# A two-layer transformer block: 64-row tile pairs in the first MLP matmul and the q/k/v projections, and a planner that charges tiling changes

## The chip, the cores and the metric

The kernel runs on one core of one Trainium2 chip. The metric is the device time of one execution in microseconds (us), from the first instruction to the last. The engines are called PE (matrix multiply; PEld is its weight loading), DVE (vector), ACT (activation functions), POOL (general) and SP (here: DMA queues only). PE multiplies a stationary operand of up to 128 rows by 128 columns with a moving operand that streams through it column by column; a matmul can also use a tile of the array: 64 of the 128 rows (64x128), 32 rows (32x128), or 32 of the columns (128x32).

## The reference

All tensors are bfloat16; `x` is 2048 rows of 576. Two layers of attention and MLP, each with the same weights:

```python
def _A_ref(x, wqkv, wo):            # 32 heads of 18, window of 256
    qkv = (x @ wqkv).reshape(B, S, 3, H, Dh).transpose(2, 0, 3, 1, 4)
    q, k, v = qkv[0], qkv[1], qkv[2]
    scores = einsum("bhqd,bhkd->bhqk", q, k) * (Dh ** -0.5)
    mask = (idx[:, None] - idx[None, :] >= 0) & (idx[:, None] - idx[None, :] < W)
    p = softmax(where(mask, scores, -1e9))
    o = einsum("bhqk,bhkd->bhqd", p, v)
    return o.transpose(0, 2, 1, 3).reshape(B, S, D) @ wo

def _B_ref(x, w1, b1, w2, b2):      # 576 -> 4608 -> 576
    h = gelu(einsum("bsd,df->bsf", layernorm(x), w1) + b1)
    return einsum("bsf,fd->bsd", h, w2) + b2

x = x + _A_ref(layernorm(x), wqkv, wo);  x = x + _B_ref(layernorm(x), w1, b1, w2, b2)
x = x + _A_ref(layernorm(x), wqkv, wo);  x = x + _B_ref(layernorm(x), w1, b1, w2, b2)
```

The contraction of the projections and of the first MLP matmul is 576 = 4 x 128 + 64, so it is four whole row blocks of the array and a half one.

## The kernel before

**Tiling.** The 2048 rows are 16 row tiles of 128, four row tiles make a chunk, and two layers make 16 / 4 x 2 = 8 chunks (`CH`, `k` = 0 to 7). Per chunk the stages are: layer norm and a transposing DMA into `xnTa` (`ln1`, `ln_norm_T`); q, k and v for each row tile (`qkv`); attention for eight groups of four heads (`E`, with `scores` and `pv`); the output projection, residual and second layer norm (`tail`, into `xnTm`); the first MLP matmul with gelu (`G_part`); the second MLP matmul (`mm2`). The MLP's 36 blocks of 128 features are done in three parts of twelve (`NPT`, `NFH`), so there are 24 calls of `G_part` and 24 of `mm2`. `hT` holds the twelve blocks of one part and is not doubled: the first MLP matmul of a part writes it through gelu, the second reads it.

**q/k/v and output projection.** `two_out` makes one row tile's 576 output columns as two halves of 288 (`HB`), each in a PSUM bank of its own, with five matmuls of 128 rows: the fifth row block has 64 rows of data and 64 rows of zeros (`wqkv[64:128, 4, :]` is zeroed at the start, and `xn` beyond column 576 too).

**First MLP matmul.** Per six feature blocks `G_part` first issues a task called `rest` (line 919): six matmuls of 64 rows each, the half row block of features 0, 3, 1, 4, 2, 5, where 0, 1, 2 lie in rows 0 to 63 of the array and 3, 4, 5 in rows 64 to 127. It opens six PSUM banks. Then each feature block gets its four whole row blocks (line 931) in its bank, and ACT applies gelu to it (line 934). To have the last 64 rows of `xnTm` in both row halves, `ln_norm_T` with `dup=True` writes them twice (line 648). After each sixth feature block a load of the next six blocks of `w1` is queued on SP (`w1_load`: one large DMA and two small; three buffers).

**Order.** Nothing is ordered by hand. `Plan.add` collects tasks with an engine, a cost, resources and a priority; `Plan.schedule` then plays them through in a model and puts each engine's instructions in the order of their planned starts. At each step it takes the task with the smallest key (start, priority, index). PE's tasks have a mode: "f" full tiles (`two_out`, `mm2`, the four whole row blocks, transposes), "h" the 64-row `rest`, "r" the 32-row scores, "c" the 32-column p·v. A task whose mode differs from the one before costs `SWITCH` = 0.095 more in the model, but the key doesn't see this. `rest` tasks may be drawn ahead by up to `HOLD` = 0.3 us. Scores and first MLP matmuls follow one fixed order ("pa"), and so do their activations on ACT ("act"); all else goes by priority. `PL.nudge` adds a number to the priority of each stage ("ea3" is the first part of attention of chunk 3, "q3.1" is q/k/v of its row tile 1, "gb2" the second MLP part of chunk 2, "+" their loads).

`Sched.add` turns resources into semaphore waits. Where a PE task writes what an earlier PE task wrote, no wait is made, since PE keeps the order of its own matmuls:

```python
lw = self.last_write.get(w)
if lw is not None and not (eng == "pe" and lw[2] == "pe"):
    want(lw)
```

PSUM has eight banks. Scores take pairs (0,1), (2,3), (4,5); q/k/v, output projection, `mm2` and p·v take one of 4 to 7 (q/k/v of chunk 1: bank 6); the first MLP matmul may take any.

Of the kernel before, what the change touches and what calls it, by code (L numbers as in the profile page):

```python
# [40 lines left out]
class Sched:  # L41
# [23 lines left out]
    def add(self, eng, fn, reads=(), writes=(), dma=None, ring=4):  # L65
# [11 lines left out]
        for w in writes:  # L77
            for rd in self.readers.get(w, ()):
                if rd[2] != eng or rd[3]:
                    want(rd[:3])  # L80
            lw = self.last_write.get(w)
            if lw is not None and not (eng == "pe" and lw[2] == "pe"):
                want(lw)
# [19 lines left out]
        own = None if dma is not None else eng  # L103
        ev = (c, c.val, own)
# [4 lines left out]
        for r in reads:  # L109
            self.readers.setdefault(r, []).append((c, c.val, own, dma is not None))  # L110
# [49 lines left out]
class Task:  # L160
    __slots__ = ("idx", "eng", "fn", "reads", "writes", "cost", "lat", "prio", "dma", "ring", "handles", "alloc", "move", "desc",
                 "npred", "succ", "ready", "end", "plain", "fifo", "hold", "stage", "mode")
# [24 lines left out]
class Plan:  # L187


    def __init__(self, S, nbanks):  # L190
        self.S = S
        self.tasks = []
        self.lw = {}
        self.rd = {}
        self.nbanks = nbanks
        self.warm_fn = None
        self.warm_from = 0.0
        self.warm_until = 0.0
        self.feed_until = 0.0
        self.hold = 0.0  # L200
        self.ring = RING
        self.stage = ""
        self.nudge = {}
        self.fifo_last = {}

    def add(self, eng, fn, reads=(), writes=(), dma=None, ring=4, cost=0.1, lat=0.1, prio=0.0, alloc=(), fifo=None, plain=False, after=(), move=0.0, desc=0, hold=False, mode="f"):
        stage = self.stage + ("+" if dma in ("w1", "w2", "xr") else "")
# [3 lines left out]
                 plain=plain, move=move, desc=desc, fifo=fifo, hold=hold, stage=stage, mode=mode)  # L211
# [31 lines left out]
    def keep_warm(self, a, b, bank_free, extra):  # L243
# [5 lines left out]
        if n < 1 or not banks:  # L249
            return  # L250
        h = Bank(())
        h.no = banks[0]
        t = Task(idx=-1, eng="pe", fn=lambda e: self.warm_fn(e, h.no, n), reads=("warm",), writes=(h,), cost=n * 0.115, lat=0.1, prio=0.0,
                 dma=None, ring=4, alloc=(), handles=(), plain=False, move=0.0, desc=0, fifo=None, hold=False, stage="", mode="f")
        extra.append((a, t))

    def schedule(self):
# [56 lines left out]
        while len(order) < n:  # L314
            best = None
            cands = []
            for e in ENGS:
                for t in released[e]:
# [7 lines left out]
                    key = (round(st, 3), t.prio, t.idx)  # L326
                    if e == "pe" and (st < self.feed_until or t.mode != "f"):
                        cands.append((key, t, st, got))
# [9 lines left out]
            if t.eng == "pe" and t.fifo is None:  # L338
                for c in cands:
                    if c[1].hold and c[2] <= st + self.hold:  # L340
                        _, t, st, got = c
            if t.eng == "pe" and mode != "f" and t.mode == "f":
                near = [c for c in cands if c[1].mode in "rc" and c[2] <= st + GLUE]
                if near:
                    _, t, st, got = min(near, key=lambda c: c[0])
# [49 lines left out]
            for s, data in t.succ:  # L395
                same = s.eng == t.eng == "pe"
# [7 lines left out]
        for st, t in order:  # L404
            names = lambda rs: [n for r in rs for n in ([f"pb{b}" for b in r.banks()] if isinstance(r, Bank) else [r])]
            if t.plain:
                self.S.plain(t.eng, t.fn)
            else:
                self.S.add(t.eng, t.fn, names(t.reads), names(t.writes), dma=t.dma, ring=t.ring)
# [6 lines left out]
GLUE = -1  # L416
WARM_UNTIL = 140.0
FEED_UNTIL = 40.0
HOLD = 0.3


def build_kernel(nc, A_x, A_wqkv, A_wo, B_x, B_w1, B_b1, B_w2, B_b2, out):
# [25 lines left out]
    PAT = (6, 6)  # L448
# [3 lines left out]
    TOPF = D - 512  # L452

# [9 lines left out]
    PL.nudge = {"b": 29.4, "ea0": -2.66, "ld0": 0.01, "ld0+": -29.79, "eb0": 0.53, "ec0": 3.31, "le0+": 114.63, "q1.0": -118.82, "q1.1":  # L463
                -98.11, "q1.2": -0.91, "q1.3": -7.44, "t0": -5.22, "ea1": -89.48, "ga0": -171.5, "ga0+": 5.04, "eb1": -15.16, "ma0": 12.04,
                "ma0+": -17.91, "gb0": -145.98, "ec1": -2.99, "le1+": 16.44, "le1": -20.83, "mb0": -3.03, "q2.1": 45.54, "q2.2": 88.61,
                "q2.3": 55.86, "t1": -120.53, "gc0": -19.84, "gc0+": -25.1, "ln3": 57.08, "mc0": 4.28, "mc0+": 148.11, "ga1": -4.06, "ga1+":
                -6.33, "eb2": -3.01, "ma1": 5.64, "ma1+": 13.09, "gb1": -0.44, "ec2": 3.21, "mb1": 7.94, "mb1+": -24.34, "q3.0": 14.13,
                "q3.1": 131.09, "q3.2": 4.89, "q3.3": 1.84, "t2": -15.58, "gc1": 7.36, "gc1+": -31.57, "mc1": 17.31, "mc1+": -1.81, "ga2":
                -27.48, "ga2+": 158.23, "eb3": 36.01, "ma2": 50.85, "ma2+": 24.11, "gb2": 23.88, "gb2+": 71.77, "ec3": -0.31, "mb2": 60.21,
                "mb2+": -145.98, "q4.0": 0.58, "q4.1": 63.81, "q4.2": 55.53, "t3": 61.03, "gc2": 154.1, "gc2+": 8.93, "ln5": 14.44, "ea4":  # L470
                19.04, "mc2": 63.19, "ga3": 18.64, "ga3+": 0.44, "eb4": 14.59, "ma3": 30.2, "ma3+": 0.16, "gb3": -9.23, "gb3+": -6.16,
                "mb3": 45.14, "q5.0": 113.74, "q5.1": 29.89, "q5.2": -8.93, "q5.3": 76.56, "t4": -2.66, "gc3": 88.61, "gc3+": -48.97, "ln6":
                -15.57, "ea5": -72.82, "mc3": -2.47, "mc3+": 76.5, "ga4+": -33.16, "eb5": 2.91, "ma4": 29, "ma4+": 17.98, "gb4": -4.52,
                "gb4+": -7.43, "mb4": 59.81, "mb4+": -8.12, "q6.0": 1.38, "q6.1": 19.98, "q6.2": -18.44, "q6.3": 63.81, "gc4": 92.87,
                "gc4+": 84.52, "ln7": 31.11, "ea6": -2.66, "mc4": 24.73, "mc4+": 0.51, "ga5": 11.4, "ga5+": 1.49, "eb6": -0.34, "ma5":
                52.45, "ma5+": -6.49, "gb5": -32.33, "gb5+": 51.26, "ec6": -3.2, "mb5": 0.24, "mb5+": -3.62, "q7.0": 24.18, "q7.2": 137.8,
                "q7.3": 1.6, "t6": -24.34, "gc5": 5.59, "gc5+": -171.5, "ea7": 41.87, "mc5": 136.49, "mc5+": -1.6, "ga6": -32.64, "eb7":
                31.31, "ma6": 44.85, "ma6+": -1.66, "gb6": 0.02, "gb6+": -4.59, "ec7": -0.12, "mb6": 104.87, "mb6+": 63.38, "t7": -16.91,
                "gc6+": -0.75, "mc6": -119.39, "mc6+": -8.02, "ga7": -61.44, "ga7+": -11.43, "ma7": -14.13, "ma7+": 9.77, "gb7": 1, "mb7":
                3.96, "mb7+": -8.3, "gc7": 53.28, "mc7": 65.68, "": 0.88}  # L480
# [92 lines left out]
    def w_load(n, reads=()):  # L573
# [3 lines left out]
        dma("act", wqkv[0:64, 4, n * D:(n + 1) * D], A_wqkv[512:576, n * D:(n + 1) * D], reads=reads, writes=[f"w{w}B"], cost=0.6, prio=-10,  # L577
            fifo="act")
# [13 lines left out]
    add("pool", lambda e: e.memset(xn[:, :, D:KD * 128], 0.0), writes=[f"xn{i}" for i in range(NXN)], cost=0.4, prio=-10)  # L592
# [4 lines left out]
    add("dve", lambda e: e.memset(wqkv[64:128, 4, :], 0.0), writes=["wqC", "wkC", "wvC"], cost=1.0, prio=-8)  # L597
# [15 lines left out]
    PL.hold = HOLD  # L613
# [104 lines left out]
    def qkv(k, i, prio0):  # L718
        l, t0, nt = CH[k]
        A = l * NT + t0 + i  # L720
        for n, w in enumerate("qkv"):
            prio = prio0 + (0.8 if k == 1 and w == "v" else 0.0) if k else QK0.get((w, i), -0.55 + 0.01 * i)
            dest = [f"v{A % VS}h{o}" for o in range(2)] if w == "v" else [f"qn{qn_ctr[0] % NQN}h{o}" for o in range(2)]
            bs = two_out(lambda c: xnTa[:, c, i * 128:(i + 1) * 128], lambda c, s, n=n: wqkv[:, c, n * D + s:n * D + s + HB],
                         [f"w{w}A", f"w{w}B", f"w{w}C", f"xa{i}"], prio + 0.01 * n, after=dest, fill=(6,) if k == 1 else FILL)
# [98 lines left out]
    def pv(k, g, units, bo, first, last, prio):  # L824

        l, t0, nt = CH[k]
        T0 = l * NT + t0

# [29 lines left out]
    def E(k, gs, prio):  # L858
# [3 lines left out]
        for g in gs:  # L862
            units = []
            bo = Bank(OUT)
            for n, parts in enumerate(us):
                units.append((parts, scores(k, g, parts, prio)))
# [6 lines left out]
        for p in pend:  # L873
            pv(k, *p[1:], prio - 0.1)

# [10 lines left out]
    def tail(k, prio):  # L886
        l, t0, nt = CH[k]
        for i in range(nt):
            t = t0 + i
            bs = two_out(lambda c, i=i: attT[:, c, i * 128:(i + 1) * 128], lambda c, s: wo_sb[:, c, s:s + HB],  # L890
# [5 lines left out]
            ln_norm_T(t, i, xnTm[:, k % 2], f"xm{k % 2}_", prio, dup=True)  # L896


    def G_part(k, hf, prio):
# [5 lines left out]
        for n4 in PAT:  # L905
            fs = range(f, f + n4)
            f += n4
            sls = [(k * NGR + ff // GS) % NB1 for ff in fs]
            bks = [Bank(MM1) for _ in fs]
            rd = [[f"w1a{sl}", f"w1b{sl}_0", f"w1b{sl}_1"] for sl in sls]  # L910

            def rest(e, sls=sls, bks=bks):

                ins = None
                for i in (0, 3, 1, 4, 2, 5):
                    sl, bk = sls[i], bks[i]
                    b = i // 3
                    col = 4 * GW + i % 3 * 128
                    ins = e.matmul(bank(bk)[:, 0:n], w1_sb[64 * b:64 * b + 64, sl, col:col + 128], xnTm[64 * b:64 * b + 64, k % 2, 4, 0:n],  # L919
                                   start=True, stop=False, tile_position=(64 * b, 0))  # L920
                return ins
            add("pe", rest, reads=list(dict.fromkeys(sum(rd, []))) + TXm, writes=bks, cost=mm_cost(n) * (n4 // 2) + 0.02, hold=True, mode="h", prio=prio,
                alloc=bks, fifo="pa", after=[f"h{ff - hf * NFH}" for ff in fs])
            for ff, sl, bk, r in zip(fs, sls, bks, rd):
                fl = ff - hf * NFH

                def fn(e, ff=ff, sl=sl, bk=bk):
                    ins = None
                    for c in range(4):
# [216 lines left out]
```

## Time and profile before

| what | value |
|---|---|
| time, three runs | 895.59, 895.8, 897.97 us; median 895.8 |
| span of the profiled execution | 895.5 us |
| granted PE clock, mean | 0.998 |
| ACT busy: exp (L798) / gelu (L934) | 345.8 / 197.8 us |
| ACT table loads | 25 and 24, 1.28 us each |
| second MLP matmul (L960), steps | 2304 of 288 columns, 309.5 us busy |
| output projection (L699, `wo_sb`) | 320 matmuls, 42.8 us busy |
| DMA | 122.25 MB, mean 137 GB/s |

"Busy" counts the time in which an engine has at least one instruction running. On PE that is little help by itself: matmuls overlap, the recorded length of one (287 ns for 288 columns) is longer than the step from its start to the next one's, and a busy engine may be between two tilings. The rows of a group name its source line; a line such as L699 is that of a helper which several stages use, so the operands (`wqkv` or `wo_sb`) tell them apart. A few matmul records are missing from the trace (1100 of 1152 on L931).

### The profile page before, as it was taken

What the parts mean: (1) busy time and instruction counts of PE and PEld (TensorE: products, weight loads), DVE (VectorE), ACT (ScalarE), POOL (GpSimd) and SP (SyncE); (2) the same over time, 40 slices, a digit from 0 to 9 for tenths busy, and PEclk for the clock granted to TensorE, in tenths of its full rate; (3) what the DMA queues carried; (4) which work ended last, traced back from release to release, by engine and by line L of the source; (5) the groups of instructions that cost most, each with busy time, mean ns of one, the idle gap of its engine ahead of it and who ended that gap; (6) DMA issues with size and microseconds to landing.
All of it is one profiled execution on the core that took longest, in us unless ns stands there. A gap on an engine that the chain in (4) does not pass through costs nothing.

```text
span 895.5 us, 19577 instructions
## 1 busy us (share of the span) xinstructions
PE 864.4 (97%) x7849; PEld 506.5 (57%) x7901; DVE 410.1 (46%) x969; ACT 615.8 (69%) x737; POOL 366.2 (41%) x504
## 2 busy tenths in 40 slices
PE   5898999999999999999999999999999999999998
PEld 4555455656566565665655655556556545556665
DVE  6789223863357351763427633375134523161111
ACT  3976888577767788366773868747777689844443
POOL 3677544274244662224431544416444266231100
PEclk9999999999999999999999999999999999999999
DMA  6788537742477333853457342682537632446431
GB/s 177 139 172 173 179 119 182 178 109 81 149 166 158 120 120 98 183 124 121 130 119 181 71 158 86 143 198 67 165 119 147 184 125 71 144 126 176 153 96 50
DMA packets 182649, 122.25 MB, mean 137 GB/s; under 512 B 107424, under 2 KB 181024, under 8 KB 182560
## 3 DMA queue, kind: packets, MB, share of 16 engines
q1 hardware_dynamic: 179152, 115.47, 49.5%
q0 software_dynamic: 1584, 3.54, 1.5%
q10 hardware_dynamic: 1824, 1.99, 0.7%
q8 instruction: 63, 1.03, 0.5%
q14 instruction: 26, 0.21, 0.1%
HBM read 91.28 MB, written 2.36 MB: 105 GB/s over the span
## 4 chain that ended last, share of the span: by engine, by line
PE 54%; DVE 1%; issue 1%; DMA 1%; ACT 1%; POOL 0%
PE ps L960 21%; PE ps L931 18%; PE ps L699 6%; PE ps L789 3%; PE ps L919 3%; PE ps L834 3%; ACT pT L798 1%; DVE x_res L880 0%; DMA xnTa<-xn 0%; DVE st_all L620 0%; DMA xnTm<-xn 0%; DVE xn L643 0%; DVE xn L648 0%; POOL rstd L633 0%; DVE xn L883 0%
## 5 line engine op out<-in xcount | busy, mean ns | idle before, releaser
L819 POOL TENSOR_SCALAR_AFFINE_SELECT pT<-pT 128x512 bf16<-128x512 bf16 (+1 forms) x368 | 283.5, 794 | 266.6 <-ACT pT L798 262.0
L798 ACT ACTIVATE pT<-ps 128x1024 bf16<-128x1024 f32 (+2 forms) x384 | 345.8, 972 | 58.3 <-PE ps L789 57.8
L934 ACT ACTIVATE hT<-ps,b1col 128x512 bf16<-128x512 f32 x288 | 197.8, 687 | 192.8 <-PE ps L931 188.3
L960 PE MATMUL ps<-w_sb,hT 128*128 128x288 bf16 x2304 | 309.5, 287 | 0.2
L960 PEld LDWEIGHTS ps<-w_sb,hT 128*128 128x128 bf16 x2304 | 213.9, 98 | 81.9 <-issue 24.9
L931 PE MATMUL ps<-xnTm,w_sb 128*128 128x512 bf16 x1100 | 255.0, 380 | 4.9 <-issue 3.2
L931 PEld LDWEIGHTS ps<-xnTm,w_sb 128*128 128x128 bf16 x1152 | 109.6, 98 | 137.0 <-issue 19.1
L880 DVE TENSOR_TENSOR x_res<-ps,x_res 128x288 f32<-128x288 f32 x216 | 95.9, 448 | 169.0 <-PE ps L960 158.4
L699 PE MATMUL ps<-wqkv,xnTa 128*128 128x288 bf16 x960 | 136.0, 289 | 3.5 <-DVE qn L742 1.9
L845 DVE STREAM_TRANSPOSE oq<-ps 128x512 f32<-128x512 f32 x64 | 45.8, 715 | 179.0 <-PE ps L834 178.8
L699 PEld LDWEIGHTS ps<-wqkv,xnTa 128*128 128x128 bf16 x960 | 88.4, 98 | 41.4 <-issue 7.8
L742 DVE CAST qn<-ps 128x288 bf16<-128x288 f32 x120 | 53.2, 449 | 35.1 <-PE ps L699 33.0
L942 POOL TENSOR_TENSOR x_res<-x_res,b2bc 128x576 f32<-128x576 f32 x32 | 40.8, 1274 | 69.2 <-ACT hT L934 69.2
L789 PE MATMUL ps<-qT,kT 32*128 32x384 bf16 (+2 forms) x1216 | 64.1, 276 | 2.2 <-ACT pT L798 2.0
L631 POOL TENSOR_SCALAR vtmp<-mv_all 128x1 f32<-128x1 f32 (+1 forms) x43 | 8.5, 197 | 121.4 <-DVE mv_all L622 120.6
L834 PE MATMUL ps<-pT,vA 128*20 128x384 bf16 (+2 forms) x1408 | 50.7, 276 | 2.0 <-ACT pT L798 0.9
L620 DVE BATCH_NORM_STATS2 st_all<-x_res 128x6 f32<-128x288 f32 x104 | 44.8, 448 | 1.2
L919 PE MATMUL ps<-xnTm,w_sb 64*128 64x512 bf16 x288 | 39.7, 381 | 5.5 <-ACT pT L798 3.3
L789 PEld LDWEIGHTS ps<-qT,kT 32*128 32x128 bf16 x1216 | 19.5, 92 | 44.1 <-issue 25.1
L699 PE MATMUL ps<-wo_sb,attT 128*128 128x288 bf16 x320 | 42.8, 286 | 0.1
L834 PEld LDWEIGHTS ps<-pT,vA 128*20 128x20 bf16 x1408 | 25.7, 90 | 26.8 <-issue 13.4
L729 DVE CAST vA<-ps 128x288 bf16<-128x288 f32 x64 | 28.8, 454 | 23.7 <-PE ps L699 23.4
(47 smaller groups left out, 347.6 us busy)
## 6 DMA issues: line engine op xcount, KB each, us to landing
w_sb<-in_B_w_dram SPq DMA_DIRECT2D x48, 864.0 KB, 5.4
w_sb<-in_B_w_dram SPq DMA_DIRECT2D x48, 768.0 KB, 4.7
w_sb<-in_B_w_dram SPq DMA_DIRECT2D x96, 48.0 KB, 4.4
x_res<-in_A_x_dram POOLq DMA_DIRECT2D x3, 1152.0 KB, 7.0
out_dram<-xn SPq DMA_DIRECT2D x16, 144.0 KB, 1.8
wqkv<-in_A_wqkv_dram ACTq DMA_DIRECT2D x3, 576.0 KB, 6.9
w_sb<-in_A_x_dram SPq DMA_DIRECT2D x2, 576.0 KB, 4.2
wo_sb<-in_A_wo_dram SPq DMA_DIRECT2D x4, 144.0 KB, 2.6
```

The lines of the kernel that those rows point to most:

```text
L699: ins = e.matmul(bank(bs[o])[:, 0:HB], lhs(c), rhs(c, o * HB), start=(c == 0), stop=(c == KD - 1))
L742: add("dve", lambda e, b=bs[o], dst=dst: e.tensor_copy(dst, heads_of(bank(b))), reads=[bs[o]], writes=[f"qn{sl}h{o}"], cost=0.375, lat=0.1 ...
L789: ins = e.matmul(two(bs[j // 2])[:, j % 2, col:col + nq * 128], k_of(T0 + so)[0][32 * j:32 * j + 32, g, :], qs[32 * j:32 * j + 32, g, qo * ...
L798: add("act", lambda e, h2=h2: e.activation(pT[:, sl, 2 * h2:2 * h2 + 2, lo:hi], two(bs[h2])[:, :, lo:hi], ACT.Exp, scale=SCALE), reads=[bs ...
L819: add("pool", lambda e, ap=ap, pat=pat, sgn=sgn, kind=kind: e.affine_select(ap, ap, pattern=pat, compare_op=(ALU.is_ge if kind == "d" else ...
L834: ins = e.matmul(bank(bo)[32 * j:32 * j + VW, qo * 128:(qo + nq) * 128], vA[:, (T0 + so) % VS, 8 * j + g, :], pT[:, sl, j, col:col + nq * ...
L845: add("dve", lambda e: e.transpose(oq[:, 0:4 * nt, :].rearrange("p b c -> p (b c)"), bank(bo)[:, 0:nt * 128]), reads=[bo, f"aq{(g - 1) % G ...
L880: add("dve", lambda e: e.tensor_tensor(x_res[:, t, sl], bank(b)[:, 0:HB], x_old[:, t, sl], ALU.add), reads=[b] + ([f"xin{t}"] if first els ...
L919: ins = e.matmul(bank(bk)[:, 0:n], w1_sb[64 * b:64 * b + 64, sl, col:col + 128], xnTm[64 * b:64 * b + 64, k % 2, 4, 0:n], start=True, stop ...
L931: ins = e.matmul(bank(bk)[:, 0:n], w1_sb[:, sl, col:col + 128], xnTm[:, k % 2, c, 0:n], start=False, stop=(c == 3))
L934: add("act", lambda e, ff=ff, fl=fl, bk=bk: e.activation(hT[:, fl, 0:n], bank(bk)[:, 0:n], ACT.Gelu_apprx_tanh, bias=b1col[:, ff:ff + 1]), ...
L960: ins = e.matmul(bank(b)[:, 0:HB], hT[:, fl, i * 128:(i + 1) * 128], w2_sb[:, fl, hh * HB:(hh + 1) * HB], start=(fl == 0), stop=(fl == NFH ...
```

## The change

The first MLP matmul and the q/k/v projections of chunks 2 to 7 (`KF = 2`) are made of 64-row tiles alone. Two outputs make a pair, each with its own bank, A and B, and the pair is worked in two tasks. In phase 0, A uses the array's rows 0 to 63 and B rows 64 to 127: the half row block first, then one half of each of the four whole row blocks, ten matmuls that alternate between the halves. In phase 1 the halves are exchanged, with the other half of each whole row block, eight matmuls. Phase 1 is added with `own=True`: `Sched.add` then makes PE wait, by semaphore, for its own phase 0 of that pair, and the planner counts phase 0's latency (0.22 us) before it. In the MLP two pairs are interleaved: phase 0 of both, then phase 1 of both; the part's twelve blocks are paired as `PAIRS` says. For q/k/v the pair is the two 288-column halves.

The half row block of `wqkv` is laid out for this: its columns for output half 0 lie in rows 0 to 63 and those for half 1 in rows 64 to 127, each with zeros opposite, so that chunks 0 and 1, which keep `two_out`, can still use it as a row block of 128. The three weight DMAs for it become six, the memset becomes two, and every layer norm now writes its last 64 columns twice (`dup=True`), which makes the memset of `xn` unnecessary. `w1_load` is queued after the second and the third group of four feature blocks instead of after blocks 5 and 11.

In the planner the key of a PE task from 40 us on gets a charge for a pair of modes (`PL.turn`); `HOLD` and `GLUE` go; `PL.nudge` has an entry for each row tile, head group or MLP group (`PL.part`), with new numbers throughout.

```diff
-    def add(self, eng, fn, reads=(), writes=(), dma=None, ring=4):
+    def add(self, eng, fn, reads=(), writes=(), dma=None, ring=4, own=False):
...
-            if lw is not None and not (eng == "pe" and lw[2] == "pe"):
+            if lw is not None and (own or not (eng == "pe" and lw[2] == "pe")):
                 want(lw)
...
-                    key = (round(st, 3), t.prio, t.idx)
-                    if e == "pe" and (st < self.feed_until or t.mode != "f"):
+                    key = (int((st + (self.turn.get(mode + t.mode, 0.0) if e == "pe" and st >= self.turn_from else 0.0)) * 1000 + 0.5), t.prio, t.idx)
+                    if e == "pe":
                         cands.append((key, t, st, got))
...
-                same = s.eng == t.eng == "pe"
+                same = s.eng == t.eng == "pe" and not s.own
...
-    PAT = (6, 6)
+    PAIRS = (((0, 3), (1, 4)), ((2, 5), (6, 9)), ((7, 10), (8, 11)))
+    KF = 2
+    PL.turn = {"ff": 0.02, "fh": 0.24, "fc": 0.44, "rf": 0.05, "rr": 0.16, "cf": 0.56, "ch": 1.05, "cr": 0.47, "cc": 0.72}
...
-        dma("act", wqkv[0:64, 4, n * D:(n + 1) * D], A_wqkv[512:576, n * D:(n + 1) * D], reads=reads, writes=[f"w{w}B"], cost=0.6, prio=-10,
-            fifo="act")
+        for b in range(2):
+            cols = slice(n * D + b * HB, n * D + (b + 1) * HB)
+            dma("act", wqkv[64 * b:64 * b + 64, 4, cols], A_wqkv[512:576, cols], reads=reads, writes=[f"w{w}B{b}"], cost=0.6, prio=-10,
+                fifo="act")
...
+            if k < KF:
+                bs = two_out(lambda c: xnTa[:, c, i * 128:(i + 1) * 128], lambda c, s, n=n: wqkv[:, c, n * D + s:n * D + s + HB],
+                             wr, prio + 0.01 * n, after=dest, fill=(6,) if k == 1 else FILL)
+            else:
+                bs = [Bank(FILL), Bank(FILL)]
+                for ph in range(2):
+                    def half(e, ph=ph, n=n, bs=bs):
+                        ins = None
+                        for c in ((4, 0, 1, 2, 3) if ph == 0 else (0, 1, 2, 3)):
+                            for o in ((0, 1) if ph == 0 else (1, 0)):
+                                r = 64 * (o ^ ph)
+                                col = n * D + o * HB
+                                ins = e.matmul(bank(bs[o])[:, 0:HB], xnTa[r:r + 64, c, i * 128:(i + 1) * 128], wqkv[r:r + 64, c, col:col + HB],
+                                               start=(c == 4), stop=(ph == 1 and c == 3), tile_position=(r, 0), skip_group_check=True)
+                        return ins
+                    add("pe", half, reads=wr, writes=bs, cost=mm_cost(HB) * (5 - ph) + 0.01, lat=0.22,
+                        prio=prio + 0.01 * n, mode="h", own=(ph == 1), alloc=(bs if ph == 0 else ()), after=(dest if ph == 0 else ()))
...
+        for gi, pairs in enumerate(PAIRS):
+            fs = [f + x for p in pairs for x in p]
...
+            for ph in range(2):
+                for u in range(2):
+                    ix = (2 * u, 2 * u + 1)
...
+                    def half(e, ph=ph, ix=ix, fs=fs, sls=sls, bks=bks):
+                        ins = None
+                        for c in ((4, 0, 1, 2, 3) if ph == 0 else (0, 1, 2, 3)):
+                            for w in ((0, 1) if ph == 0 else (1, 0)):
+                                i = ix[w]
+                                r = 64 * (w ^ ph)
+                                g = fs[i] % GS
+                                col = 4 * GW + g % 3 * 128 if c == 4 else c * GW + g * 128
+                                ins = e.matmul(bank(bks[i])[:, 0:n], w1_sb[r:r + 64, sls[i], col:col + 128], xnTm[r:r + 64, k % 2, c, 0:n],
+                                               start=(c == 4), stop=(ph == 1 and c == 3), tile_position=(r, 0), skip_group_check=True)
+                        return ins
+                    bb = [bks[i] for i in ix]
+                    add("pe", half, reads=rd + TXm, writes=bb, cost=mm_cost(n) * (5 - ph) + 0.01, mode="h", prio=prio,
+                        lat=0.22, alloc=(bb if ph == 0 else ()), fifo="pa", own=(ph == 1),
+                        after=([f"h{fs[i] - f}" for i in ix] if ph == 0 else ()))
...
+            if gi:
+                w1_load(prio - 2)
...
-            ln_norm_T(t, i, xnTa, "xa", prio)
+            ln_norm_T(t, i, xnTa, "xa", prio, dup=True)
```

## The prediction

> **What bounds the kernel.** I read the page first: busy times, then the slices, to see whether one engine carries the span.
>
> ```profile
> PE 864.4 (97%) x7849; PEld 506.5 (57%) x7901; DVE 410.1 (46%) x969; ACT 615.8 (69%) x737; POOL 366.2 (41%) x504
> PE   5898999999999999999999999999999999999998
> ```
>
> PE is full in nearly every slice, ACT has 280 us to spare. But a busy PE may be switching instead of streaming, so I asked the groups of PE with shapes kept apart, and then PE's instructions in order of time.
>
> ```profile
> L931 PE MATMUL ps<-xnTm,w_sb 128*128 128x512 bf16 x1100 | 255.0, 380 | 4.9 <-issue 3.2
> L699 PE MATMUL ps<-wqkv,xnTa 128*128 128x288 bf16 x960 | 136.0, 289 | 3.5 <-DVE qn L742 1.9 <-DVE oq L845 0.6 <-DMA xnTa<-xn 0.5
> L919 PE MATMUL ps<-xnTm,w_sb 64*128 64x512 bf16 x288 | 39.7, 381 | 5.5 <-ACT pT L798 3.3 <-DVE xn L643 1.0 <-DMA xnTm<-xn 0.4
> ```
>
> ```profile
> 448.65 1.67 PE L931 MATMUL ps<-xnTm,w_sb 128*128 128x512 bf16 x7
> 450.25 0.82 PE L919 MATMUL ps<-xnTm,w_sb 64*128 64x512 bf16 x6
> 451.01 1.25 PE L931 MATMUL ps<-xnTm,w_sb 128*128 128x512 bf16 x5
> ...
> 459.81 1.64 PE L960 MATMUL ps<-w_sb,hT 128*128 128x288 bf16 x12
> 461.38 0.29 PE L789 MATMUL ps<-qT,kT 32*128 32x256 bf16 x4
> ```
>
> Columns: start, length, engine, line, count. Matmuls overlap their ends, so the price of one is the step from start to start. L931: (1.67 - 0.38) / 6 = 0.215 us. L960: (1.64 - 0.287) / 11 = 0.123 us, and L699 has the same 288 columns. L919 is six 64-row matmuls, in three pairs: the two of a pair start 3 ns apart, and 0.82 - 0.38 leaves 0.44 for two pair steps, 0.22 each (0.2155 from the start times). So two 64-row tiles on opposite row halves cost what one full tile costs. A tiling change: the last L931 starts at 448.65 + 1.67 - 0.38 = 449.94 and the first L919 0.31 later, 0.095 over the step; the way back costs 0.093; L960 to L789 is 461.38 - (459.81 + 1.64 - 0.287) = 0.217 against 0.123, again 0.095. In order of time PE's matmuls make 247 stretches of full tiles, 192 of scores, 64 of p·v and 48 of the 64-row "rest": 550 changes, 550 x 0.095 = 52 us. Steps without changes or waits add up to some 801 us. So the end is set by PE's steps, then its tiling changes, then about 31 us without any matmul (895.5 - 864.4), 9.1 of them before the first.
>
> **Part by part.** The sum is made against 895.5, the span of the profiled execution; the median of the runs shown, 895.8, is 0.3 above.
>
> 1. First MLP matmul. Before: 1152 full matmuls and 288 half ones in 144 pairs, 1296 steps of 0.2155. After: 24 parts x 12 features x 9 half matmuls = 2592 in 1296 pairs. Streaming changes by 0. Weight loads rise from 1440 to 2592; in the rest, the second load of a half starts 11 ns after that half's matmul and takes 94 ns of a 215 ns step, so they hide. If that cover went, it is 0.094 a pair (a rival below).
>
> 2. q/k/v of chunks 2 to 7. 960 x 6/8 = 720 full steps become 72 output pairs x 9 = 648 pair steps: -72 x 0.1225 = **-8.8**. No trace row has a pair at 288 columns. Bounds: the nearest rows are L919 (two halves for one full step, -8.8) and, if nothing is gained, 0.136 a pair (0). I take -8.8, since 11 + 94 ns of a load fit into 122 ns.
>
> 3. Tiling changes. The 48 rests go, and with them 96 edges. Come: 24 MLP parts x 2 edges = 48; q/k/v, two output pairs to a visit as the four banks 4 to 7 allow, 36 visits x 2 = 72 edges, of which I let half fall on an edge to a score that is there anyway: 36. The charge in the order (none from scores to p·v, 0.44 from full tiles to p·v) should bring some 20 more p·v next to a score. -96 + 48 + 36 - 20 = -32, x 0.095 = **-3.0**. Bounds: all new edges hidden beside scores and 77 saved at p·v -173 (-16); all of them paid, every part cut once more, none saved at p·v, +72 (+7).
>
> 4. Banks at an MLP part's start. The rest takes six banks at once, the new half two, and the second pair two more. That wait is in PE's list:
>
> ```profile
> PE ps L919 <- ACT pT L798: 3.3, 3, 1.5
> PE ps L919 <- DVE xn L643: 1.0, 1, 1.0
> ```
>
> The first goes: **-3.3** (bounds -3.3 and 0, if the next need of banks waits instead); the second, for the normalised rows, stays.
>
> 5. Features finish in pairs. Before, a gelu's bank is done each 0.86 us; after, the last two of a part together. End of a part in the late stage:
>
> ```profile
> 832.19 11.41 PE L960 MATMUL ps<-w_sb,hT 128*128 128x288 bf16 x90
> 832.39 0.69 ACT L934 ACTIVATE hT<-ps,b1col 128x512 bf16<-128x512 f32 x1 [0.18 <-PE ps L931]
> 833.09 1.28 ACT L975 ACT_TABLE_LOAD   x1
> 833.13 10.16 PEld L960 LDWEIGHTS ps<-w_sb,hT 128*128 128x128 bf16 x84 [0.35 <-ACT hT L934]
> ```
>
> Six matmuls of the second MLP (0.735) run from 832.19, then PE waits for the last gelu: next load 833.13, 0.21 lost. After: counted from 832.19, the second last pair is ready at 0.20 - 4 x 0.2155 = -0.66, the last at 0.20; four gelus in a row at 0.61 (the closest two in the trace) to 0.69 start at -0.66, -0.05 to 0.03, 0.56 to 0.72, 1.17 to 1.41, the last ends at 1.86 to 2.10. PE loses 1.15 to 1.4, so about 1.0 more. From 800 us on there are four such ends with nothing else to run: **+4**. At the other 20, scores and p·v stand behind the part (456.29 to 457.17 is 0.88 us of them), so 0.15 each, **+3** (bounds 0, and 20 with no cover). Late next would be the gelu table's change back and the next exps, but ACT has slack.
>
> 6. The wait of phase two for phase one, on PE itself. Everything in PE's order stands behind it: scores (for them ACT), p·v, second MLP. In the MLP the other pair lies between, 5 or 4 steps, 1.08 or 0.86 us; a matmul record outlasts its step by 0.165 and restart after a signal takes some 0.05 (gelu end 833.08 to load 833.13), 0.22 in all: covered. In q/k/v the cover is another half (0.49 to 0.61 us) if banks are free: 72 x 0.22 = 16 at worst, 0 at best; I take one in six, **+2.5**.
>
> 7. Small steps at no cost: 32 more copies of 64 columns on DVE (L648, 0.31 each, 10 us of DVE's 485 idle); they sit before a transposing DMA whose row tile is needed a chunk later. In the first chunk they stand ahead of PE's first matmul at 9.13: **+0.4** (0 to 1.2, four of them). Three more weight DMAs at ACT's start: six take 3.62 us, nine end at 6.2, the table load (1.28) at 7.5, ACT's first copy is at 9.88: covered. The zeroing of the weights' tail is the same bytes in two pieces. The w1 loads on SP are as many as before (one large, two small), some 1.1 us later (32 steps into a part instead of 27); a slot is read again 12 features, at least 11.6 us, on and landing takes 5.4: covered. The bias additions on POOL (41% busy) wait for gelus 1.5 us later, due a part later.
>
> 8. Priorities by part and the charge in the order. Idle PE that is neither the head (9.1), the end (some 3) nor already counted (3.3) is about 16 us. I take **-6** (bounds -16, and +4 where the new order meets waits like the list's largest two).
>
> Sum: -8.8 - 3.0 - 3.3 + 4 + 3 + 2.5 + 0.4 - 6 = -11.2; 895.5 - 11.2 = 884.3, with the 0.3 some **884.5**.
>
> **A rule that speaks against it.** In the rest, the load for a half starts 11 ns after the same half's matmul, while that streams, and the pair step stays 0.2155. The Trainium skill (TensorE: Matmul & The Clock Gate, Part 3, The mechanism) says weight loads overlap running matmuls only where the row groups differ; by it every pair here would stand still for its loads and the change would lose far more than it saves. By the row the sum stays as it is; three pairs a rest do not bear the rule out.
>
> **Rivals.**
> - *The new order swallows more* (0.23): ends of parts fully covered (-3), phase waits covered (-2.5), edges and waits halfway to their lower bounds (-6 and -2): 884.5 - 13.5 = 871. For it: ACT at 69% lets work be shifted. Against: waits left in the list are short and many.
> - *Phase waits uncovered* (0.07): all 72 stall, 884.5 + 16 - 2.5 = 898. For it: a pair now holds two of four banks together until both phases are done. Against: short scores fit between.
> - *The 288-column pair is no quicker* (0.05): 884.5 + 8.8 = 893.3.
> - *The other side: gelus bunched at each part's end* (0.08). Place: second MLP behind the first, all 24 ends. Price 1.0 each, 20 more ends uncovered: 884.5 + 20 - 3 = 901.5. It decides against the change once some 14 of the 20 are uncovered. For it: in the late stage it is certain. Against: 0.88 us of other tiles behind the part at 456.
> - *Weight loads do not hide behind the same half* (0.02): (1296 + 648) x 0.094 = 183, so 1067. Against: the rest's steps.
> - The forecast itself 0.55, its own range 877 to 891.
>
> **Numbers.** About 0.3% (2.7 us) is what can be told from no change. Faster: 0.55 + 0.23 + 0.03 from the middle rivals' low sides = 0.81; same 0.07, slower 0.12, from the uncovered waits, the unquickened pair, the bunched gelus and the loads. Range 866 to 898: it leaves out the loads, most of the bunched gelus and the lower tail of the first rival, under 2 in 10.
>
> **What would show it.** In the changed profile the q/k/v group has 64-row matmuls of 288 columns, 1296 of them, pairs 0.1225 apart; if 0.136 or more, step 2 is wrong. The first MLP's pairs stay 0.2155 apart; if near 0.31, step 1. Stretches of 64-row tiles some 55 to 70 and changes about 520; more than 600 sinks step 3. Late in the run PE waits about 1.2 us for gelus at four places (step 5). Waits of 64-row matmuls for PE itself above 5 us would sink step 6. The prediction is wrong as a whole if PE's idle time grows by over 10 us.

## The result and the profile after

| kernel | median, us | runs, us | ratio to before, 95% interval |
|---|---|---|---|
| before | 897.5 | 895.6 to 899.5, five | |
| changed | 891.6 | 889.0 to 893.1, five | 0.9937, 0.9912 to 0.9961 |

The change makes the kernel faster by 0.6%, some 5.7 us. That is inside the range and on the side that was forecast, but half of the 11.2 us of the sum. The profiled execution of the changed kernel has a span of 891.0 us. The busy times and slices, as before:

```profile
PE 859.2 (96%) x9632; PEld 504.5 (57%) x9632; DVE 412.7 (46%) x1002; ACT 595.4 (67%) x737; POOL 370.2 (42%) x503
PE   5888999999999999999999999999999999999998
```

PE is 5 us less busy and still bounds the kernel, but the third slice, 45 to 67 us, has gone from 9 to 8: the start of the run is thinner. The groups of PE by shape (line, operation, tile, operands, count, busy and mean, idle before):

```profile
L996 PE MATMUL ps<-xnTm,w_sb 64*128 64x512 bf16 x2592 | 290.1, 376 | 1.5 <-DVE rinv L916 1.1 <-ACT pT L865 0.4
L788 PE MATMUL ps<-wqkv,xnTa 64*128 64x288 bf16 x1296 | 94.7, 285 | 0.7 <-DVE qn L809 0.3 <-ACT pT L865 0.2
L750 PE MATMUL ps<-wqkv,xnTa 128*128 128x288 bf16 x240 | 36.7, 296 | 4.3 <-DVE qn L809 1.3 <-DVE vA L796 0.9 <-DVE b1col L1080 0.9
```

The counts are the planned ones: 2592 and 1296 half matmuls, and 240 whole ones in chunks 0 and 1. Their steps follow from stretches of PE in order of time:

```profile
447.73 8.15 PE L996 MATMUL ps<-xnTm,w_sb 64*128 64x512 bf16 x74
...
460.80 2.38 PE L788 MATMUL ps<-wqkv,xnTa 64*128 64x288 bf16 x36
463.11 0.29 PE L856 MATMUL ps<-qT,kT 32*128 32x256 bf16 x4
```

74 matmuls are 37 pairs: (8.15 - 0.376) / 36 = 0.216 us a pair. 36 of the q/k/v are 18 pairs: (2.38 - 0.285) / 17 = 0.123 a pair. Both are the step of one full tile of that width. So the streaming went as forecast; what went otherwise stands in PE's waits:

```profile
PE ps L856 <- DMA kT<-qn: 3.5, 1, 3.5
PE ps L1033 <- ACT hT L1005: 2.6, 4, 0.8
PE ps L856 <- ACT pT L865: 1.8, 4, 1.0
PE ps L1033 <- DMA w_sb<-in_B_w_dram: 1.4, 1, 1.4
...
PE ps L996 <- ACT pT L865: 0.4, 2, 0.2
```

The wait of the first MLP for banks (3.3 us before) is down to 0.4. New are one wait of 3.5 us of the scores for a transposed row tile of kT, and the second MLP's waits for the last gelus of a part.

To see where the time between the first and the last matmul went, I took every step from one start to the next apart: columns / 2.4 ns plus 2.5 ns is streaming, up to 0.1 us at a change of tiling is the change, the rest is called idle, with what the matmuls lose where PE's clock is halved (before, 52 missing records are put in at 0.2158 us each). The last two columns are further executions, explained below.

| us | before | changed | changed, second profile | x_late |
|---|---|---|---|---|
| span | 895.5 | 891.0 | 885.4 | 882.8 |
| streaming | 801.2 | 792.5 | 792.5 | 792.5 |
| changes of tiling, number | 550 | 513 | 513 | 513 |
| changes of tiling, time | 53.9 | 50.3 | 50.1 | 50.3 |
| idle up to 110 us | 13.1 | 22.2 | 18.5 | 15.4 |
| idle after 110 us | 14.7 | 13.7 | 11.8 | 12.3 |

Streaming fell by 8.7, changes by 3.6; 9.1 us of this were given back as idle time in the first eighth of the run (5.4 in the second profile). The place, in order of time:

```profile
71.53 0.97 POOL L609 DMA_DIRECT2D x_res<-in_A_x_dram  x1
...
73.14 1.26 SPq L828 DMA_TRANSPOSE kT<-qn  x1
...
73.89 3.23 PE L750 MATMUL ps<-wo_sb,attT 128*128 128x288 bf16 x25
...
74.49 5.07 SPq L828 DMA_TRANSPOSE qT<-qn  x1
...
80.65 0.51 PE L856 MATMUL ps<-x_res 32*128 32x384 bf16 x4 [3.53 <-DMA kT<-qn]
...
81.31 1.94 ACT L865 ACTIVATE pT<-ps 128x1024 bf16<-128x1024 f32 x2 [11.78 <-PE ps L856]
```

At 71.5 POOL issues the first load of `x_res` (1152 KB). The transposes queued on SP at 73.1 and later run beside it. PE runs out of work at 77.1 (73.89 + 3.23) and waits until 80.65; ACT ran out long before and waits until 81.31. More comes on top of the wait; stretches of 5 us, PE's clock in the third column from the end:

```profile
75.00:80.00 5.00, 2.11 (x18) 1.46 (x15) 4.21 (x13) 0.00 (x0) 1.51 (x4) 0.97 1.58 256
80.00:85.00 5.00, 4.35 (x32) 1.85 (x33) 0.00 (x0) 1.94 (x2) 1.68 (x2) 0.50 0.70 119
85.00:90.00 5.00, 4.93 (x65) 2.63 (x65) 4.40 (x12) 2.69 (x3) 1.94 (x5) 0.85 0.28 56
```

From 79.7 to 86.5 the clock is halved. The q/k/v pairs there are 0.24 us apart instead of 0.123, and the matmuls of this stretch take 2.5 us longer in all.

### The profile page after: what moved, and what is told of

Read it like the earlier page. It is cut to its first block, busy times and chain, and to the rows that moved or that the text cites. A ratio compares the mean times of both kernels' runs of the same rounds, so it can differ in the third digit from the quotient of the medians.

```text
span 891.0 us, 23052 instructions
## 1 busy us (share of the span) xinstructions
PE 859.2 (96%) x9632; PEld 504.5 (57%) x9632; DVE 412.7 (46%) x1002; ACT 595.4 (67%) x737; POOL 370.2 (42%) x503
## 4 chain that ended last, share of the span: by engine, by line
PE 82%; DMA 5%; ACT 4%; DVE 3%; issue 3%; POOL 2%; ACTq 1%; POOLq 0%; DVEq 0%
PE ps L996 30%; PE ps L1033 29%; PE ps L788 8%; PE ps L856 5%; PE ps L750 5%; PE ps L902 4%; ACT pT L865 2%; POOL pT L886 2%; ACT hT L1005 1%; DMA xnTm<-xn 1%; DMA qT<-qn 1%; DMA kT<-qn 1%; DVE xn L694 1%; DMA xnTa<-xn 1%; DMA w_sb<-in_B_w_dram 1%
## 5 line engine op out<-in xcount | busy, mean ns | idle before, releaser
L886 POOL TENSOR_SCALAR_AFFINE_SELECT pT<-pT 128x512 bf16<-128x512 bf16 (+1 forms) x368 | 287.0, 804 | 308.7 <-ACT pT L865 305.5
L1005 ACT ACTIVATE hT<-ps,b1col 128x512 bf16<-128x512 f32 x288 | 175.3, 688 | 211.2 <-PE ps L996 210.6
L996 PE MATMUL ps<-xnTm,w_sb 64*128 64x512 bf16 x2592 | 290.1, 376 | 1.5 <-DVE rinv L916 1.1
L996 PEld LDWEIGHTS ps<-xnTm,w_sb 64*128 64x128 bf16 x2592 | 127.4, 94 | 145.0 <-issue 7.4
L788 PE MATMUL ps<-wqkv,xnTa 64*128 64x288 bf16 x1296 | 94.7, 285 | 0.7 <-DVE qn L809 0.3
L809 DVE CAST qn<-ps 128x288 bf16<-128x288 f32 x120 | 49.7, 449 | 67.0 <-PE ps L788 58.0
L788 PEld LDWEIGHTS ps<-wqkv,xnTa 64*128 64x128 bf16 x1296 | 59.9, 94 | 33.2 <-issue 5.3
L750 PE MATMUL ps<-wqkv,xnTa 128*128 128x288 bf16 x240 | 36.7, 296 | 4.3 <-DVE qn L809 1.3
L796 DVE CAST vA<-ps 128x288 bf16<-128x288 f32 x64 | 26.3, 450 | 30.8 <-PE ps L788 28.2
L694 DVE TENSOR_SCALAR xn<-x_res,mv_all,rstd 128x576 bf16<-128x576 f32 x52 | 32.7, 633 | 14.7 <-DMA xnTm<-xn 5.2
```

Source lines behind the costliest of these rows:

```text
L750: ins = e.matmul(bank(bs[o])[:, 0:HB], lhs(c), rhs(c, o * HB), start=(c == 0), stop=(c == KD - 1))
L788: ins = e.matmul(bank(bs[o])[:, 0:HB], xnTa[r:r + 64, c, i * 128:(i + 1) * 128], wqkv[r:r + 64, c, col:col + HB], start=(c == 4), stop=(ph ...
L809: add("dve", lambda e, b=bs[o], dst=dst: e.tensor_copy(dst, heads_of(bank(b))), reads=[bs[o]], writes=[f"qn{sl}h{o}"], cost=0.375, lat=0.1 ...
L886: add("pool", lambda e, ap=ap, pat=pat, sgn=sgn, kind=kind: e.affine_select(ap, ap, pattern=pat, compare_op=(ALU.is_ge if kind == "d" else ...
L996: ins = e.matmul(bank(bks[i])[:, 0:n], w1_sb[r:r + 64, sls[i], col:col + 128], xnTm[r:r + 64, k % 2, c, 0:n], start=(c == 4), stop=(ph == ...
L1005: add("act", lambda e, ff=ff, fl=fl, bk=bk: e.activation(hT[:, fl, 0:n], bank(bk)[:, 0:n], ACT.Gelu_apprx_tanh, bias=b1col[:, ff:ff + 1]), ...
```

## The experiments

My theory after the result: steps 2 and 3 are right, and what is missing is idle time near 80 us. Rivals: the tiles themselves cost it (phase waits, bunched gelus, banks), or their gain is smaller than the traces say.

**The changed kernel again.** No edit.

> The changed kernel once more, for a second profile and for pairing with the runs beside it. If the wait of 3.6 us for the kT transpose at 80.65 us and the half clock after it belong to this order of work, they stand here again, at 80 to 81 us, and the time is 889 to 893. If they are an accident of one execution, PE's idle time between 40 and 110 us falls from 15 to some 9 us and the span is about 885 to 887.

889.7 us, ratio 0.9936 (0.9918 to 0.9954). The wait is there again, 3.0 us at 79.6, so it belongs to this order of work. The half clock isn't: at 80 to 85 us the clock is 1.00, idle from 40 to 110 us is 11.9 us, and this execution's span is 885.4. Nor is the wait of 1.4 us for `w_sb` there, which stood at 116.7 in the first profile. Whether the halved clock follows differs from execution to execution: of the six here, the two with a mean clock of 1.000 took 887.5 and 888.2 us, the one with 0.996, as in the first profile, 892.5.

**The load moved away from the transposes.**

```diff
+        m = next(x for x in order if x[1].dma == "xr")
+        order.remove(m)
+        order = sorted(order + [(130.0, m[1])], key=lambda x: x[0])
         self.order = order
```

> The changed kernel with its first x_res load (1.2 MB on POOL's queue, issued at 71.5 us) issued some 60 us later; nothing else in any engine's order differs. Theory A (the missing gain lies in the start, where this load holds up the transposes of kT and qT and PE then runs at half clock): the wait at 80.65 and the half clock go, PE's idle time from 40 to 110 us falls from 15 to about 9 us, and the time falls by 3 to 6 us against the changed kernel beside it, to 885 to 888. Theory B (the new tiling itself costs what is missing): within 1 us of the changed kernel. If the late load only moves the collision, a new wait of some us stands between 125 and 145 us.

886.4 us, ratio 0.9900 (0.9883 to 0.9917), 3.3 us under the changed kernel beside it. The same place in its trace, PE in order of time:

```profile
75.80 0.53 PE L753 MATMUL ps<-wo_sb,attT 128*128 128x288 bf16 x3
76.26 0.34 PE L859 MATMUL ps<-x_res 32*128 32x384 bf16 x4
76.44 0.22 PE L859 MATMUL ps<-x_res,kT 32*128 32x128 bf16 x4
76.59 0.79 PE L791 MATMUL ps<-wqkv,xnTa 64*128 64x288 bf16 x10
```

No wait is left: the scores that stood until 80.65 start at 76.26. The kT transpose that PE waited for, issued at 73.14 in the changed kernel, took 7.5 us from its issue to landing, and the one before it 8.9; without the load these two, issued at 71.99 and 69.97, take 3.3 and 4.1. The one that PE waited for, in the list of DMA issues (us to landing at the end), changed kernel first:

```profile
kT<-qn SPq DMA_TRANSPOSE x1, 7.5
...
kT<-qn SPq DMA_TRANSPOSE x1, 3.3
```

Idle from 40 to 110 us is 9.1. Four of the five executions have a mean clock of 1.000, of the changed kernel's eleven three; so part of the 3.3 us is a halved clock that follows less often. No wait above 0.3 us stands between 125 and 145 us.

**The control: the same move in the kernel before.** The same edit.

> The kernel before with its first x_res load (issued at 70.7 us there) issued some 60 us later, nothing else in any engine's order differing: the control for x_late. If the collision is the changed kernel's own loss (before, PE has other work while the transposes are late), this is within 1.5 us of the kernel before, ratio 0.998 to 1.002. If the load costs the kernel before as much, about 3 us faster, ratio 0.997 or less, and the collision explains nothing of the difference between the two.

895.3 against 896.0 us, ratio 0.999 (0.998 to 1.0). There the load runs beside transposes as well (the three issued just after it land in 5 to 6 us, so the delay is shorter), but PE has other work. Its order at that place:

```profile
72.87 1.39 PE L699 MATMUL ps<-wo_sb,attT 128*128 128x288 bf16 x10
74.19 0.40 PE L789 MATMUL ps<-x_res,kT 32*128 32x256 bf16 x8
74.52 2.62 PE L699 MATMUL ps<-wo_sb,attT 128*128 128x288 bf16 x20
77.08 0.34 PE L789 MATMUL ps<-x_res 32*128 32x384 bf16 x4
77.25 0.22 PE L789 MATMUL ps<-x_res,kT 32*128 32x128 bf16 x4
```

Scores stand between the projections; in the changed kernel the projections run first, 25 matmuls on end, and then nothing is left. The load is the same; the new order takes the cover away. No run tells how much of the difference is the cover and how much the shorter delay.

**q/k/v as full tiles, at the same places.**

```diff
-                        for c in ((4, 0, 1, 2, 3) if ph == 0 else (0, 1, 2, 3)):
-                            for o in ((0, 1) if ph == 0 else (1, 0)):
-                                r = 64 * (o ^ ph)
...
+                        for c in range(KD):
+                            ins = e.matmul(bank(bs[ph])[:, 0:HB], xnTa[:, c, i * 128:(i + 1) * 128], wqkv[:, c, n * D + ph * HB:n * D + (ph + 1) * HB],
+                                           start=(c == 0), stop=(c == KD - 1))
```

> The changed kernel with the q/k/v projections of chunks 2 to 7 as full tiles at the same places in PE's order: phase 0 is the whole of output half 0, phase 1 the whole of half 1, five matmuls each. If step 2 is right, this adds 72 x 0.1225 = 8.8 us of streaming; the tiling changes rise from 513 to 560 by a count over the order, 47 x 0.095 = 4.5 us; together 13 us slower than the changed kernel, some 904. If the 288-column pairs save nothing, only the 4.5 us of changes show, some 896.

903.6 us, ratio 1.0085 (1.0057 to 1.0113): 13.8 us above the changed kernel beside it, 13 expected. The same piece of work as above, in its trace:

```profile
465.59 0.40 PE L853 MATMUL ps<-qT,kT 32*128 32x384 bf16 x8
465.92 2.62 PE L785 MATMUL ps<-wqkv,xnTa 128*128 128x288 bf16 x20
468.48 0.29 PE L853 MATMUL ps<-qT,kT 32*128 32x256 bf16 x4
```

Two output pairs are 20 steps here and 18 there, 2.62 against 2.38 us. The traces count 560 changes here and 513 there; at 0.095 each these 47 are 4.5 of the 13.8 us, and the 72 steps more the rest. Step 2 stands, size and cause.

**No exchange of halves, no wait of phase 1.**

```diff
-                                r = 64 * (o ^ ph)
+                                r = 64 * o
...
-                                r = 64 * (w ^ ph)
+                                r = 64 * w
...
-                self.S.add(t.eng, t.fn, names(t.reads), names(t.writes), dma=t.dma, ring=t.ring, own=t.own)
+                self.S.add(t.eng, t.fn, names(t.reads), names(t.writes), dma=t.dma, ring=t.ring)
```

> The changed kernel with phase 1 in the same row halves as phase 0, so that PE need not wait for itself; the other halves of the four whole row blocks are left out and these are taken twice, the work and its order are the same. If the waits of phase 1 for phase 0 are covered as the trace reads (three gaps of 0.23 us and a few of 0.05 in the q/k/v, none in the MLP), about 1 us faster than the changed kernel; by the forecast's step 6, 2.5 us faster; if they hold PE up in ways that the gaps don't show (loads that can't run ahead), 5 us or more.

This kernel takes one half of each whole row block twice and leaves the other out. 889.0 us, ratio 0.9933 (0.9916 to 0.9949), against 0.9936: nothing that can be told from the changed kernel, to within some 2 us by the two intervals. PE's wait for itself is covered, nearly everywhere.

**What the priority table is worth, and whether the tiles bring idle time.** Before and after with the table emptied:

```diff
+    PL.nudge = {}
```

> The kernel before with every entry of the priority table taken out. Shows what its table is worth, for comparison with the changed kernel treated the same way. A count over the order gives 557 tiling changes (550 with the table), so what is lost is PE's idle time: some 900 to 910 us.

> The changed kernel with every entry of the priority table taken out, the charge for tiling changes kept. Theory A (tiles and order gain only together: in an order that was not made for it, a pair that holds two banks through two phases and gelus that come in pairs leave PE idle): slower than before_plain by 5 us or more, with 586 tiling changes by a count over the order and PE idle far above 36 us. Theory B (the tiles gain by themselves, the table brings little of it): faster than before_plain by some 8 us or more.

910.6 us (ratio 1.0173, 1.0149 to 1.0197) and 923.4 us (1.0302, 1.0283 to 1.0322). By the numbers given, this was theory A: the new tiles are slower by 13 us in an order not made for them. But the planner differs too, so I took the tiles apart within the new planner (`PL.turn` emptied, and the old `G_part` loop or `KF = 8` put back):

> The changed kernel without priority table and without the charge, and with the old tiles (rest and whole row blocks in the MLP, q/k/v as full tiles): what is left of the change is the planner without its drawing ahead of the rest, and the doubled copies. Theory A (the new tiles bring PE's idle time): near before_plain, 908 to 913 us. Theory C (without a table the order that the planner falls into is a matter of chance, by some 15 us, whatever the tiles): 918 us or more, PE idle as much as in after_plain.

> As plain_old_tiles, but with the MLP's pairs. Theory A: slower than plain_old_tiles by 5 us or more. Theory C: its time says nothing of the tiles and may as well be faster; if it is under 915 us the MLP's pairs can't be what brings the idle time.

> after_plain without the charge for tiling changes: both kinds of pairs, no table. Changes fall from 586 to 534 by a count over the order, 5 us less. Theory A: PE's idle time stays where it was in after_plain, so some 918 us. Theory C: idle time moves by as much as the changes save, 920 to 927 us.

> plain_old_tiles with the charge. Changes fall from 556 to 527 by a count over the order, 2.8 us less. If the charge only saves changes, some 3 us faster than plain_old_tiles; if it pays for them with waits, no faster.

| tiles, table empty | charge | us | changes | idle, us |
|---|---|---|---|---|
| old, old planner | no | 910.6 | 557 | 34 |
| old | no | 926.0 | 556 | 48 |
| old | yes | 924.8 | 527 | 49 |
| MLP pairs, q/k/v full | no | 910.9 | 531 | 37 |
| both pairs | no | 926.9 | 534 | 62 |
| both pairs | yes | 923.4 | 586 | 51 |

(Idle as in the table above, by the same taking apart; missing records of whole row blocks put in.) Theory A falls: the old tiles in the new planner are as slow as the new ones, and the MLP's pairs alone are 15 us faster than that. Without a table the order falls out one way or another by some 15 us, which is more than the whole change. So an edit that makes the planner order anew doesn't measure the tiles; `qkv_full`, which keeps the order, does. The charge saves 29 changes with the old tiles, 2.8 us by their price; 1.3 us of it arrive, less than the two runs of each can tell from nothing.

**More to run while the last gelus finish.** On top of `x_late`:

```diff
-                    add("pe", fn, reads=[f"h{fl}" for fl in range(f0, f0 + 6 if f0 or i + hh == 0 else NFH)] + ...
+                    add("pe", fn, reads=[f"h{fl}" for fl in range(f0, f0 + 6 if f0 or i + hh == 0 or (k == NK - 1 and 2 * i + hh < 3) else NFH)] + ...
```

> x_late, and in the last chunk the first three of the second MLP's eight sums per part may start on features 0 to 5 before the last gelus are done (so far only the first may). If the stall at the end of a part in the late stage is the bunched gelus (step 5: some 0.98 us at each of three places after 800 us), two more runs of six matmuls, 1.47 us, cover it and the time falls by 2.5 to 3 us against x_late, to 883 to 884. If something else ends last there, for instance PSUM banks that are not free, less than 1 us.

The end of a part in the late stage of the changed kernel:

```profile
823.70 2.11 PE L996 MATMUL ps<-xnTm,w_sb 64*128 64x512 bf16 x18
...
824.99 2.42 ACT L1005 ACTIVATE hT<-ps,b1col 128x512 bf16<-128x512 f32 x4 [1.46 <-PE ps L996]
...
825.74 0.91 PE L1033 MATMUL ps<-w_sb,hT 128*128 128x288 bf16 x6
...
827.43 1.28 ACT L1049 ACT_TABLE_LOAD   x1
...
827.46 4.71 PE L1033 MATMUL ps<-w_sb,hT 128*128 128x288 bf16 x37 [0.81 <-ACT hT L1005]
```

Six matmuls last from 825.74 to 826.48 (6 x 0.123); the four gelus end at 827.41, and PE goes on at 827.46: 0.98 us lost. With the edit:

```profile
817.47 1.83 ACT L1008 ACTIVATE hT<-ps,b1col 128x512 bf16<-128x512 f32 x3
817.74 1.59 SPq L612 DMA_DIRECT2D w_sb<-in_B_w_dram  x3
817.76 8.49 PE L1036 MATMUL ps<-w_sb,hT 128*128 128x288 bf16 x68
```

PE runs through (68 matmuls in 8.49 us, no gap). 883.2 us, ratio 0.9869 (0.9847 to 0.9891): 3.2 us under `x_late` (2.8 by the two ratios, whose intervals just touch; the three gaps that went are 2.9), 12 to 13 under the kernel before. It beats both kernels.

## Why the prediction was right and wrong

*Step 1, streaming of the first MLP 0:* right. The pair step is 0.216 over 36 pairs on end, and loads hide although each half is reloaded at every pair.

*Step 2, -8.8:* right, by the streaming in the table and by `qkv_full`.

*Step 3, -3.0 by 32 changes less:* right in size, 37 less, 3.6 us, but the split was partly luck. There are 63 stretches of 64-row tiles, 55 to 70 were forecast; 16 of them hold q/k/v and first MLP together, which the count had as separate. The 20 edges between p·v and full tiles that the charge was to save did go (72 to 52), but not to scores (51 before, 53 after): p·v now stands beside 64-row tiles (5 before, 21 after).

*Step 4, -3.3:* right in size, 2.9: the wait for banks fell from 3.3 to 0.4 us. That fewer banks at once are the cause is argued; no run here separates it from the new order. One of the three old waits, 1.6 us at 726, was followed by a halved clock from 728.3 to 731.7, with matmuls of 512 columns 0.427 us apart; step 4 had that at nothing, and it is gone too.

*Step 5, +7:* too much. The stall is real and `x_late_fill` removes it, but it is 0.98 us at three places and 0.37 at the fourth, against 0.21 at each before: +2.5, for +4. The size was off because four gelus on end take 2.42 us, (2.42 - 0.69) / 3 = 0.58 each; I had 0.61 to 0.69. The +3 for the ends in the middle isn't seen: idle after 110 us fell.

*Step 6, +2.5:* nothing in `no_exchange`; three gaps of 0.23 us in the trace. The first bound, 0, was nearer than one in six.

*Step 7, +0.4 at the head:* the first matmul starts at 8.97 instead of 9.13, so nothing. But "covered" for the DMAs was said from their number and distance alone; which transfer runs beside which in the new order I had not asked, and the largest single loss is there.

*Step 8, -6:* this is the step that failed. I took the 16 us in which PE was idle beside the head, the end and what step 4 had counted, and let the new order cut more than a third. I had not asked where they stood: of 27.8 us between the first and last matmul, 13.1 lie before 110 us, where, as I read the order, chunks 0 and 1 offer little else to run (2.8 of them are lost by the matmuls before the clock first rises, at 14.9 us). The new order made this stretch longer, not shorter: 18.5 to 22.2 us. Over the whole run, the 27.8 us less step 4's 2.9 and with step 5's 2.5 would be 27.4. Measured are 35.9 and 30.3 in the two profiles, so step 8 came out at +8.5 and +2.9, not -6. In `x_late` 27.7 are left, step 8 at +0.3: even without the collision the new order saved no idle time, and the collision of the load with the transposes comes on top, 3.3 us in the medians, shown by `x_late` and its control. In `x_late` the early stretch still has 15.4, 2.3 more than before; between 15 and 70 us it idles 9.9 us where 6.0 were before, in waits of at most 1.2 us, and the cause stays open. Steps 5 and 6, taken too dear by some 7 us together, hid the size of this error: that the time ended inside the range is partly luck.

Of the rivals, *the new order swallows more* had two of its conditions come true, the covered phase waits and the covered ends in the middle of the run, but the idle time went the other way. *Phase waits uncovered* and *gelus bunched at each part's end* fell (the second is true in the late stage only), *the 288-column pair is no quicker* fell by `qkv_full`, and *weight loads do not hide behind the same half* by the pair steps: a stretch of 37 pairs, each half reloaded for every matmul, shows no added time. So the rule quoted from the Trainium skill (TensorE: Matmul & The Clock Gate, Part 3, The mechanism) does not hold for these tiles as I read it; the same section also lets a load run ahead into a background weight buffer, and that fits these steps. What ended on the costly side was none of the rivals: a transfer that was hidden before and isn't in the new order.

## What to carry to other kernels

Two 64-row tiles on opposite halves stream like one full tile (0.216 us a pair at 512 columns, 0.123 at 288), so a contraction of 4.5 row blocks costs 4.5 steps instead of 5; this gain can be counted beforehand, and was. When a change also makes a planner order everything anew, don't credit the new order with idle time before looking at which stretch it stands in, and look there for transfers that lose their cover. To measure the tiles alone, swap them at fixed places in the order.

## What the runs showed of the hardware that I had not expected

PE's clock halves after a short stop, and the length of the stop doesn't decide it. In the changed kernel 3.6 us without a matmul were followed by 6.8 us at half clock, in `qkv_full` 2.9 us by the same 6.8, in the kernel before a longest stop of 1.6 us by 3.4; in the second profile of the changed kernel 3.0 us were followed by none.

The traces show a grid behind this. In all fourteen profiles the clock changes only at whole multiples of 3.41 us after its first rise. Stretches of this grid, cut out one by one (the first figure after the length is PE's busy time); the changed kernel:

```profile
76.31:79.72 3.41, 0.80 (x7) 0.40 (x5) 2.94 (x10) 0.00 (x0) 1.51 (x4) 1.00 1.66 200
79.72:83.13 3.41, 2.48 (x21) 1.17 (x22) 0.00 (x0) 1.82 (x2) 0.00 (x0) 0.50 1.13 197
83.13:86.55 3.42, 3.42 (x25) 1.30 (x22) 1.54 (x5) 0.12 (x1) 1.70 (x2) 0.50 0.00 0
```

Its second profile, where the stop lies across two stretches:

```profile
74.49:77.90 3.41, 2.18 (x18) 1.50 (x16) 3.37 (x10) 0.00 (x0) 0.76 (x2) 1.00 2.06 340
77.90:81.32 3.42, 1.68 (x23) 0.93 (x23) 0.91 (x4) 1.23 (x2) 0.75 (x2) 1.00 1.03 175
81.32:84.73 3.41, 3.35 (x47) 1.92 (x47) 2.61 (x8) 2.27 (x3) 2.43 (x4) 1.00 0.42 82
```

And the kernel before:

```profile
724.84:728.26 3.42, 1.61 (x18) 0.76 (x18) 2.24 (x5) 3.42 (x4) 2.42 (x3) 1.00 0.98 301
728.26:731.67 3.41, 3.08 (x10) 1.04 (x8) 0.00 (x0) 2.32 (x3) 1.60 (x4) 0.50 0.74 258
```

Counted by matmul steps (columns / 2.4 ns plus 2.5 ns each), a full-clock stretch was followed by half clock 19 times in the fourteen profiles. Each of these had steps for at most 0.37 of its time (the busy time is longer, since a record outlasts its step); of the 3574 that were followed by full clock all but one (0.36) had 0.39 or more. So what counts in these runs is how little PE does within one stretch of the grid, and where a stop falls on the grid differs from execution to execution (the clock's first rise comes 12.4 to 15.6 us after the start). The Trainium skill (TensorE: Matmul & The Clock Gate, Part 1) says that the clock is set by a free-running window of some 3.4 us; the 3.41 us of the traces agree, and 6.8 us is two such windows.

A transposing DMA that takes 3.3 us to land without the load took 7.5 us beside a 1152 KB load from another queue.
